# First quad's v brought to token order by four transfers from the scalar engine's queue instead of by TensorE, with all instructions in another order

## The chip, the cores and the metric

The kernel runs on one core of one Trainium2 chip. The metric is the device time of one execution in microseconds (us); less is better. The core has five instruction streams: TensorE (PE in the profile, its weight loads PEld), VectorE (DVE), ScalarE (ACT), GpSimd (POOL) and SyncE (SP). SP, ACT and POOL can each issue DMA transfers; the profile calls the DMA queue of SP q1, that of ACT q10 and that of POOL q0. Differences below about 0.3% (0.5 us) cannot be told from no change by a measurement of this kernel.

## The reference

```python
B, H, S, D = 4, 8, 768, 48
f = 1.0 / (1.0 + np.exp(-f_logit))
for t in range(S):
    state = f[:, :, t, :, None] * state + einsum('bhd,bhde', k[:, :, t], v[:, :, t])
    y[:, :, t] = einsum('bhd,bhde->bhe', q[:, :, t], state)
x = y.transpose(0, 2, 1, 3).reshape(3072, 384)
h = x @ w_in                       # 384 -> 2048
out = maximum(0.01 * h, h) @ w_out # 2048 -> 384
```

A gated linear attention over 768 tokens for four batches of eight heads is followed by a two-layer feed-forward block with a leaky ReLU.

## The kernel before

The sequence is cut into six chunks of 128 tokens. A chunk of one batch is a unit, numbered u = 4c + b, and the four units of a chunk are called a quad here. For each quad the kernel loads f, k, q and v, turns the gates into cumulated logarithms and from them into two factors, scales k and q by them, computes scores, masks them to the causal half, multiplies them with v ("mix"), adds the part that comes from the state, and updates the state. The result x of a unit feeds the feed-forward: `up` (x times w_in, L468, and L478 for later quads), the leaky ReLU on ScalarE (L473, L482), and `down` (times w_out, L486).

All instructions are written out by hand in one list of calls, in an order that holds for every engine: an engine runs its own instructions in the order of the list and waits on semaphores for what it needs. The DMA queue of an engine follows that engine's instructions. Tiles are fixed, with no allocator that could reorder anything.

The first quad is special. Its tokens are loaded interleaved: partition p holds batch p // 32 and four neighbouring tokens (32 times 4 = 128 tokens of a batch). Scaling and turning (`q_turn_pe`, `q_k_mul` and `q_q_mul`, L262 and L267) bring k and q into token order, and the scores come out in token order (`q_score_pe`, L281). The masks are made by VectorE (`q_mask`, L292), or by a ScalarE copy (`q_wf_act`, L285) and a GpSimd select (`q_mask_pool`, L288). v must be in token order too, 128 tokens of one batch on 128 partitions in tile `v_b`, before `q_mix_pe` (L307) and `state_pe` (L444) can use it. In the kernel before, two casts (`q_v_cast`) make v bf16, TensorE multiplies it for each batch with four 0/1 matrices `pick` (`q_pick`, L252: four matmuls for each batch, sixteen in all), and four copies (`q_v_out`) bring the result out of PSUM. Later quads use `cast_v` into the tile `vQ` and `v_dma`, one SBUF-to-SBUF transfer for each batch, from SP's queue (L391).

Calls to `idle_pe` put matmuls on zeros (L140) into PE's order where it has nothing to do; they are not part of the computation. `load_w_in` and `load_w_out` (L181, L186) load the feed-forward weights in four pieces each from POOL's queue, with a cast to bf16 on the way. `load_all` loads one chunk of an input, 768 KB, from SP's queue. `gate` is a one-element write that keeps a load from starting before its buffer is free.

Of the kernel before, what the change touches and what calls it, by code (L numbers as in the profile page):

```python
# [16 lines left out]
def kernel(  # L17
# [10 lines left out]
    nc = tc.nc  # L28
# [141 lines left out]
    def clear(eng, what):  # L170
        t = {"k": khQ[1][:, :, D:64], "q": qhQ[1][:, :, D:64], "v": vQ[:, :, :, D:64],
             "b": vbu[0][:, :, :, D:64]}[what]
        eng.memset(t, 0.0)
# [72 lines left out]

    def q_v_cast(eng, hh):
        move(eng, vqb[:, 4 * hh:4 * hh + 4], vq[:, 4 * hh:4 * hh + 4])

    def q_pick(b, bk):  # L250
        for i in range(4):
            nc.tensor.matmul(bank(bk)[:, 0:H * D].rearrange("p (h d) -> p h d", h=H),  # L252
                             pick[:, b, i].rearrange("p t j -> p (t j)"), vqb[:, :, i, :], start=(i == 0), stop=(i == 3))
# [132 lines left out]
    def cast_v(eng, c, hh):  # L386
        h = slice(4 * hh, 4 * hh + 4)
        move(eng, vQ[:, :, h, 0:D], v_raws[c % len(v_raws)][:, h].rearrange("p h j d -> p j h d"))

    def v_dma(c, b):  # L390
        nc.sync.dma_start(out=vbu[c % 2][:, b].rearrange("p h d -> p (h d)"),  # L391
                          in_=vQ[b::B].rearrange("p j h d -> p j (h d)"))
# [118 lines left out]
    clear(G, 'v')  # L511
    q_exp_act(0)
    q_exp_act(1)
# [3 lines left out]
    q_gate32(0, 0, 1, 2, 3)  # L517
    q_decay_b(0, emT, 1.0, 0, 0)
    idle_pe(2, 7)
    q_gate32(1, 0, 1, 2, 3)  # L520
    gate(G, fqs[0])
    gate(G, fqs[1])
    q_decay_b(1, emT, 1.0, 1, 0)
    q_k_cast(V, 0)
    load_all(fqs[1], f_logit, 1)
    q_decay_b(0, emT, 1.0, 0, 1)
    q_k_cast(V, 1)
    q_decay_b(1, emT, 1.0, 1, 1)
    idle_pe(4, 7)
    q_turn_pe(khq, 0, 4)  # L530
    load_all(fqs[0], f_logit, 2)
    q_decay_b(0, aT, -1.0, 0, 1)
    clear(V, 'b')
    q_decay_b(0, aT, -1.0, 0, 0)
    q_turn_pe(khq, 1, 5)
    q_k_mul(0, 1, 0, 4)
    q_decay_b(3, emT, 1.0, 3, None)
    q_k_mul(0, 0, 0, 4)
    q_decay_b(2, emT, 1.0, 2, None)
    q_k_mul(1, 0, 0, 5)  # L540
    q_q_cast(V, 1)
    q_q_cast(G, 0)
    q_decay_b(3, aT, -1.0, 3, None)
    q_k_mul(1, 0, 1, 5)
    q_decay_b(2, aT, -1.0, 2, None)
    idle_pe(11, 7)
    q_turn_pe(qhq, 1, 0)
    q_k_mul(0, 0, 1, 4)
    q_decay_b(1, aT, -1.0, 1, 0)
    touch('k')  # L550
    q_k_mul(1, 1, 1, 5)
    q_turn_pe(qhq, 0, 2)
    q_decay_b(1, aT, -1.0, 1, 1)
    q_k_mul(0, 1, 1, 4)
    q_q_mul(1, 1, 0, 0)
    q_back_pe(3, 4)
    q_q_mul(0, 1, 1, 2)
    q_back_pe(2, 1)
    q_v_cast(G, 0)
    q_v_cast(A, 1)  # L560
    q_q_mul(1, 0, 0, 0)
    q_q_mul(1, 1, 1, 0)
    q_q_mul(0, 0, 1, 2)
    q_q_mul(1, 0, 1, 0)
    load_w_in(1)
    idle_pe(8, 7)
    q_score_pe(0, 1, 3, 6)
    q_k_mul(1, 1, 0, 5)
    q_score_pe(1, 1, 0, 7)
    q_wf_act(0, 1, 1, 6)  # L570
    q_back_out(V, 3, 4)
    q_back_pe(1, 5)
    load_w_in(0)
    q_mask(0, 1, 0, 3)
    q_pick(1, 4)
    q_back_out(A, 2, 1)
    q_q_mul(0, 1, 0, 2)
    q_mask_pool(0, 1, 1)
    q_wf_act(1, 1, 1, 7)
    order_pe(3)  # L580
    q_q_mul(0, 0, 0, 2)
    q_pick(2, 1)
    q_mask(1, 1, 0, 0)
    load_w_in(2)
    q_v_out(A, 1, 4)
    g_exp(1, 0)
    q_score_pe(0, 0, 7, 2)
    q_v_out(V, 2, 1)
    q_score_pe(1, 0, 0, 4)
    q_mask_pool(1, 1, 1)  # L590
    q_pick(3, 6)
    order_out(3)
    q_wf_act(1, 0, 1, 4)
    load_w_in(3)
    clear(V, 'q')
    q_pick(0, 3)
    q_mask(0, 0, 0, 7)
    q_v_out(A, 3, 6)
    q_mask_pool(1, 0, 1)
    q_wf_act(0, 0, 1, 2)  # L600
    q_mix_pe(2, 4)
    gate(V, qqs[1])
    q_mask(1, 0, 0, 0)
    load_all(qqs[1], q, 1)
    q_mix_pe(3, 7)
    x_out(A, 2, 4)
    q_back_pe(0, 6)
    q_mask_pool(0, 0, 1)
    q_v_out(V, 0, 3)
    state_pe(3, 2)  # L610
    g_exp(2, 1)
    x_out(V, 3, 7)
    load_w_out(0)
    idle_pe(2, 1)
    q_mix_pe(1, 3)
    q_mix_pe(0, 4)
    g_exp(1, 1)
    q_back_out(V, 0, 6)
    up(1, 3, 7)
    x_out(V, 1, 3)  # L620
    g_ln(1, 0)
    x_out(V, 0, 4)
    up(1, 2, 6)
    q_back_out(V, 1, 5)
    g_exp(2, 0)
    up(0, 2, 4)
    q_state_dve(3)
    g_ln(2, 1)
    up(1, 0, 5)
    up(1, 1, 2)  # L630
    g_ln(1, 1)
    up(0, 3, 3)
    g_ln(2, 0)
    g_sum(V, 1, 1)
    up(0, 0, 0)
    up_act(1, 1, 2)
    g_sum(V, 1, 2)
    up(1, 5, 1)
    up_act(1, 3, 7)
    gate(V, kqs[1])  # L640
    g_sum(V, 1, 3)
    load_all(kqs[1], k, 1)
    up_act(1, 0, 5)
    up(0, 5, 2)
    g_sum(V, 2, 1)
    g_cast(G, 1)
    up_act(0, 3, 3)
    load_all(v_raws[0], v, 1)
    state_pe(1, 5)
    clear(V, 'k')  # L650
    up_act(0, 0, 0)
    g_pe(1, 7)
    g_sum(V, 2, 2)
    up(1, 4, 3)
    up_act(1, 5, 1)
    g_sum(V, 2, 3)
    up_act(0, 2, 4)
    state_pe(0, 0)
    up(0, 4, 1)
    up_act(1, 2, 6)  # L660
    g_add(1, 1, 7)
    g_cast(G, 2)
    up(0, 1, 4)
    up_act(0, 5, 2)
    load_w_out(1)
    q_state_dve(1)
    up_act(0, 4, 1)
    g_pe(2, 6)
    up(0, 6, 2)
    up_act(1, 4, 3)  # L670
    g_add(1, 0, 7)
    up_act(0, 1, 4)
    state_pe(2, 5)
    up(1, 6, 3)
    g_a(1, 1)
    q_state_dve(0)
    up(0, 7, 4)
    g_a(1, 0)
    q_state_dve(2)
    down(3, 0, 0)  # L680
    g_em(1, 0)
    g_q(V, 1, 0)
    q_state_pool(2)
    down(2, 0, 5)
    g_q(V, 1, 2)
    up_act(1, 6, 3)
    up(1, 7, 1)
    g_end(1, 7)
    q_state_pool(0)
    up_act(0, 6, 2)  # L690
    g_q(V, 1, 3)
    down(1, 0, 7)
    g_em(1, 1)
    g_q(V, 1, 1)
    t_pe(1, 1, 1, 2)
    q_state_pool(3)
    g_k(V, 1, 1)
    up_act(0, 7, 4)
    down(0, 0, 3)
    g_end(2, 6)  # L700
    g_k(V, 1, 0)
    up_act(1, 7, 1)
    t_pe(1, 1, 0, 4)
    load_w_out(2)
    t_out(A, 1, 1, 1, 2)
    g_k(V, 1, 3)
    t_pe(1, 0, 0, 1)
    load_w_out(3)
    g_add(2, 0, 6)
    down(2, 1, 5)  # L710
    t_out(A, 1, 0, 0, 1)
    down(3, 1, 0)
    g_k(V, 1, 2)
    t_out(V, 1, 1, 0, 4)
    kq_dma(1, 0, 3)
    t_pe(1, 0, 1, 2)
    cast_v(G, 1, 1)
    down(0, 1, 3)
    kq_dma(1, 0, 0)
# [641 lines left out]
```

## Time and profile before

| | |
|---|---|
| median of 3 runs | 175.36 us (175.34 to 175.89) |
| the profiled execution | 176.12 us, of which the span from the first to the last instruction is 174.4 us |
| PE busy | 168.3 us (96% of the span) |
| DVE busy | 109.2 us (63%) |
| ACT busy | 110.8 us (64%) |
| POOL busy | 49.9 us (29%) |
| moved by DMA | 37.53 MB, mean 215 GB/s |

The span is the profiled execution's time without what lies before its first and behind its last instruction, 1.7 us here. Busy matmuls on PE include those on zeros (10.3 us). In the timeline a row gives start, duration, engine, line, operation, output and input, the count, and in brackets the idle time just ahead of it with what ended it. In the DMA view a row gives a queue's packets, megabytes, and share of 16 engines' time in the stretch asked for.

### The profile page before, as it was taken

The page shows a single profiled execution, that of the slowest core. Times are in us where ns is not written, and L with a number is a line of the kernel's source. Part 1 is how long each engine was busy: PE and PEld are TensorE (multiplying, and loading weights), DVE is VectorE, ACT ScalarE, POOL GpSimd, SP SyncE. Part 2 cuts the span into 40 slices and gives each one's busy share as a digit, 9 for nine tenths or more (in the row PEclk, how much of TensorE's full clock was granted, in tenths as well). Part 3 has the DMA queues.
Part 4 walks back from the last instruction along what each step waited for, and adds up shares of the span by engine and source line. Part 5 has one row for each costly group of instructions (what it writes and reads, how often), then busy time and mean ns, then how long its engine had stood idle before and what let it go on. Part 6 is the DMA issues. An engine that isn't in the chain of part 4 may idle for free.

```text
span 174.4 us, 4660 instructions
## 1 busy us (share of the span) xinstructions
PE 168.3 (96%) x1896; PEld 108.4 (62%) x1896; DVE 109.2 (63%) x230; ACT 110.8 (64%) x201; POOL 49.9 (29%) x99
## 2 busy tenths in 40 slices
PE   7999999999999999999999999999999999999992
PEld 5776699866664566575555755555655566555572
DVE  7789959899766688966399768759470472020000
ACT  2786899994189997278982397790449703366531
POOL 7227803473003393000690002184038100000000
PEclk9999999999999999999999999999999999999999
DMA  5999999979499998999995999867699540007222
GB/s 152 302 327 319 198 208 296 317 126 233 126 344 331 333 235 164 346 260 355 212 237 146 341 240 300 238 165 242 165 282 195 157 167 4 0 0 272 89 92 93
DMA packets 52917, 37.53 MB, mean 215 GB/s; under 512 B 16416, under 2 KB 52384, under 8 KB 52896
## 3 DMA queue, kind: packets, MB, share of 16 engines
q1 hardware_dynamic: 50160, 33.69, 70.3%
q0 software_dynamic: 2176, 3.15, 10.6%
q10 hardware_dynamic: 560, 0.39, 0.8%
q8 instruction: 15, 0.25, 0.6%
q14 instruction: 6, 0.05, 0.1%
HBM read 25.17 MB, written 4.72 MB: 171 GB/s over the span
## 4 chain that ended last, share of the span: by engine, by line
PE 68%; ACT 9%; DMA 8%; DVE 7%; SPq 4%; issue 2%; POOL 0%; ACTq 0%; DVEq 0%
PE ps L486 29%; PE ps L478 24%; DMA qq<-in_q_dram 6%; ACT gT L473 3%; PE ps L420 3%; DMA fq<-in_f_logit_dram 2%; SPq L391 2%; PE ps L436 2%; PE ps L432 2%; PE ps L252 2%; PE ps L491 2%; DVE qhQ L377 1%; PE ps L444 1%; ACT fq L341 1%; ACT fq L337 1%
## 5 line engine op out<-in xcount | busy, mean ns | idle before, releaser
L486 PE MATMUL ps<-w_out_b,gT 128*128 128x384 bf16 x368 | 66.3, 326 | 0.0
L478 PE MATMUL ps<-xQ,w_in 128*128 128x512 bf16 x240 | 56.1, 379 | 0.4 <-ACT osb L146 0.4
L482 ACT ACTIVATE gT<-ps 128x512 bf16<-128x512 f32 x80 | 42.8, 611 | 17.2 <-PE ps L478 16.8
L486 PEld LDWEIGHTS <-gT 128*128 128x128 bf16 x368 | 34.4, 98 | 23.2
L478 PEld LDWEIGHTS <-w_in 128*128 128x128 bf16 x240 | 26.5, 113 | 21.8 <-issue 0.6
L424 DVE TENSOR_TENSOR wm<-ps,ut 128x512 bf16<-128x512 f32 x40 | 24.8, 682 | 12.0 <-ACT gT L482 6.8
L146 ACT CAST xQ<-ps 128x384 bf16<-128x384 f32 x14 | 6.1, 482 | 21.1 <-PE ps L436 21.0
L329 POOL CAST sb<-sf 64x192 bf16<-64x192 f32 x40 | 17.5, 436 | 4.9 <-DVE sf L323 2.5
L458 POOL TENSOR_TENSOR sf<-sf,a_end 128x192 f32<-128x192 f32 x16 | 9.3, 581 | 28.0 <-DVE sf L453 18.0
L146 ACT COPY osb<-ps 128x384 f32<-128x384 f32 (+1 forms) x15 | 6.8, 456 | 13.3 <-PE ps L486 8.6
L377 DVE TENSOR_TENSOR qhQ<-qq,a_t 128x384 bf16<-128x384 f32 x20 | 11.7, 617 | 2.0 <-DMA qq<-in_q_dram 1.6
L377 DVE TENSOR_TENSOR khQ<-kq,em_t 128x384 bf16<-128x384 f32 x20 | 11.8, 622 | 1.7 <-DMA kq<-in_k_dram 1.0
L361 DVE TENSOR_TENSOR fq<-fq,ps 128x768 f32<-128x768 f32 x10 | 9.4, 952 | 4.6 <-ACT gT L482 2.7
L468 PE MATMUL ps<-xQ,w_in 128*128 128x256 bf16 x96 | 11.5, 273 | 0.0
L140 PE MATMUL ps<-fill 128*128 128x256 bf16 x66 | 10.3, 318 | 1.1 <-DVE fill L97 1.1
L148 POOL CAST vQ<-v_raw 128x768 bf16<-128x768 f32 x8 | 6.9, 873 | 14.9 <-DMA v_raw<-in_v_dram 14.7
L148 DVE COPY osb<-ps 128x384 f32<-128x384 f32 x10 | 5.4, 554 | 9.0 <-PE ps L486 8.8
L345 DVE TENSOR_TENSOR fq<-fq 128x384 f32<-128x384 f32 x15 | 8.8, 592 | 2.7 <-issue 1.7
L148 POOL CAST lfq<-fq 128x384 bf16<-128x384 f32 x4 | 2.1, 529 | 29.1 <-ACT gT L482 16.6
L468 PEld LDWEIGHTS <-w_in 128*128 128x128 bf16 x96 | 10.1, 114 | 0.2
L452 DVE TENSOR_TENSOR sf<-sf,ps 64x192 f32<-64x192 f32 x16 | 5.5, 344 | 7.5 <-PE ps L444 7.2
L365 ACT ACTIVATE em_t<-fq 128x768 bf16<-128x768 f32 x10 | 8.7, 874 | 0.4 <-DVE fq L361 0.4
(100 smaller groups left out, 196.7 us busy)
## 6 DMA issues: line engine op xcount, KB each, us to landing
kq<-in_k_dram SPq DMA_DIRECT2D x6, 768.0 KB, 7.2
qq<-in_q_dram SPq DMA_DIRECT2D x6, 768.0 KB, 7.6
fq<-in_f_logit_dram SPq DMA_DIRECT2D x5, 768.0 KB, 7.3
v_raw<-in_v_dram SPq DMA_DIRECT2D x5, 768.0 KB, 6.3
out_dram<-osb SPq DMA_DIRECT2D x4, 768.0 KB, 4.0
kh<-khQ SPq DMA_DIRECT2D x20, 128.0 KB, 5.0
v_b<-vQ SPq DMA_DIRECT2D x20, 128.0 KB, 2.1
w_in<-in_moe_w_in_dram POOLq DMA_DIRECT2D x4, 384.0 KB, 7.6
```

The costliest lines, as they stand in the source:

```text
L140: nc.tensor.matmul(bank(bk)[:, 0:256], fill[:, 0:128], fill[:, 0:256], start=True, stop=True)
L146: eng.copy(out=out, in_=in_)
L148: eng.tensor_copy(out=out, in_=in_)
L329: nc.gpsimd.tensor_copy(out=state_b[b][r, :, e * D:(e + 1) * D], in_=state_f[b][r])
L361: nc.vector.tensor_add(t, t, x[:, :, None, :].to_broadcast([128, 4, 4, D]))
L377: eng.tensor_mul(out.rearrange("p (j g) d -> p j g d", j=4)[:, :, h, 0:D], raw[:, h].rearrange("p e j d -> p j e d"), by[:, h].rearrange(" ...
L424: nc.vector.tensor_mul(wms[e][u % R_WM], bank(bk).rearrange("p (i n) -> p i n", i=P2), ut[:, None, :].to_broadcast([128, P2, 128]))
L458: nc.gpsimd.tensor_mul(sf, sf, a_ends[c % 2][:, :, b:b + 1].to_broadcast([128, P2, D]))
L468: nc.tensor.matmul(bank(bk)[:, i * 256:(i + 1) * 256].rearrange("p (a n) -> p a n", a=2), w_in_p[ff // 4][:, kk, :, ff % 4], xQs[0][:, 2 * ...
L478: nc.tensor.matmul(bank(bk).rearrange("p (a n) -> p a n", a=B), w_in_p[ff // 4][:, kk, :, ff % 4], xQs[c % R_XT][:, :, kk, :], start=(kk = ...
L482: nc.scalar.activation(g_piece(c, ff), bank(bk), AF.Prelu, alpha=0.01)
L486: nc.tensor.matmul(bank(bk)[:, 0:KD], g_part(u, ff), w_out_b[:, ff, :], start=(ff == 0), stop=(ff == NF - 1))
```

## The change

The functions `q_v_cast`, `q_pick` and `q_v_out` go, and with them the tile `pick`, its building on GpSimd and VectorE, and the clearing of the padding of `v_b`. The first quad uses `cast_v` like the others, from the tile `vq`, and `v_dma` gets an argument for the issuing engine, which is ScalarE for the first quad. The list of calls is in another order throughout.

```diff
-    spare = gTs[GBUFS - 4].rearrange("p f a n -> p (f a n)")
-    vqb = spare[:, 2048:2048 + H * 4 * D].rearrange("p (h j d) -> p h j d", h=H, j=4)
-    pick = spare[:, 0:2048].rearrange("p (b i t j) -> p b i t j", b=B, i=4, j=4)
-    nc.gpsimd.memset(pick, 0.0)
-    for i in range(4):
-        nc.vector.tensor_copy(out=pick[:, :, i, :, i], in_=ident.rearrange("p (t b) -> p b t", b=B))
...
-    def q_v_cast(eng, hh):
-        move(eng, vqb[:, 4 * hh:4 * hh + 4], vq[:, 4 * hh:4 * hh + 4])
-
-    def q_pick(b, bk):
-        for i in range(4):
-            nc.tensor.matmul(bank(bk)[:, 0:H * D].rearrange("p (h d) -> p h d", h=H),
-                             pick[:, b, i].rearrange("p t j -> p (t j)"), vqb[:, :, i, :], start=(i == 0), stop=(i == 3))
-
-    def q_v_out(eng, b, bk):
-        move(eng, v_bs[b][:, :, 0:D], bank(bk)[:, 0:H * D].rearrange("p (h d) -> p h d", h=H))
...
     def cast_v(eng, c, hh):
         h = slice(4 * hh, 4 * hh + 4)
-        move(eng, vQ[:, :, h, 0:D], v_raws[c % len(v_raws)][:, h].rearrange("p h j d -> p j h d"))
-
-    def v_dma(c, b):
-        nc.sync.dma_start(out=vbu[c % 2][:, b].rearrange("p h d -> p (h d)"),
+        t = v_raws[c % len(v_raws)] if c else vq
+        move(eng, vQ[:, :, h, 0:D], t[:, h].rearrange("p h j d -> p j h d"))
+
+    def v_dma(c, b, eng=nc.sync):
+        eng.dma_start(out=vbu[c % 2][:, b].rearrange("p h d -> p (h d)"),
                           in_=vQ[b::B].rearrange("p j h d -> p j (h d)"))
...
+    load_w_out(0)
...
+    v_dma(0, 0, A)
+    q_q_mul(1, 1, 0, 1)
+    load_w_in(2)
```

ScalarE's instructions in the first quad, before, from its half of the cast of v on (`gT_173` and `gT_174` are the tiles lent to v, `wm` the masked scores, `v_b_160` v in token order for all four batches, `fq_72` the gates of the second chunk, `xQ_170` the x of the first quad):

```order
L146 CAST gT_173<-gT_174 128x768
L285 CAST wm_167<-ps_67 128x512
L146 COPY kh_154<-ps_62 128x512
L285 CAST wm_169<-ps_68 128x512
L146 CAST v_b_160<-ps_65 128x8x48
L337 ACTIVATE fq_72<-fq_72 128x768
L285 CAST wm_168<-ps_65 128x512
L146 CAST v_b_160<-ps_67 128x8x48
L285 CAST wm_166<-ps_63 128x512
L146 CAST xQ_170<-ps_65 128x384
```

The same stretch of ScalarE in the changed kernel:

```order
L146 CAST vQ<-gT_174 128x4x4x48
L267 CAST wm_167<-ps_63 128x512
L374 DMA v_b_160<-vQ 128x1x512 x2
L267 CAST wm_166<-ps_67 128x512
L374 DMA v_b_160<-vQ 128x1x512 x2
L267 CAST wm_168<-ps_67 128x512
L267 CAST wm_169<-ps_63 128x512
L319 ACTIVATE fq_72<-fq_72 128x768
L323 ACTIVATE fq_72<-fq_72 128x768
L146 CAST xQ_170<-ps_65 128x384
```

The four transfers stand between the copies of the scores, the first two behind the first copy; both gate activations of the second chunk now stand ahead of the copy of x.

GpSimd's instructions before, from the building of the constants on (`four` is a small constant, `gT_173` in its second appearance the target of the cast of v, `w_in_100` to `w_in_102` pieces of the first weights):

```order
L209 COPY four<-ident 4x128
L213 MEMSET gT_173 128x2048
L173 MEMSET vQ 128x32x16
L166 CAST fq_71<-ident 128x1
L166 CAST fq_72<-ident 128x1
L148 CAST qhQ_111<-qq_75 128x16x48
L177 COPY seen<-kq_73 128x1
L148 CAST gT_173<-gT_174 128x768
L181 DMA w_in_101<-in_moe_w_in_dram 128x3x512
L181 DMA w_in_100<-in_moe_w_in_dram 128x3x512
```

The same stretch of GpSimd in the changed kernel:

```order
L208 COPY four<-ident 4x128
L185 DMA w_out_b<-in_moe_w_out_dram 128x1536
L148 CAST khQ_109<-kq_73 128x16x48
L166 CAST fq_72<-ident 128x1
L176 COPY seen<-kq_73 128x1
L148 CAST qhQ_111<-qq_75 128x16x48
L180 DMA w_in_101<-in_moe_w_in_dram 128x3x512
L148 CAST vQ<-gT_174 128x4x4x48
L180 DMA w_in_100<-in_moe_w_in_dram 128x3x512
L180 DMA w_in_102<-in_moe_w_in_dram 128x3x512
```

The first piece of w_out stood behind the masks of the first quad, as the fifth weight load; it is now the first transfer of POOL's queue, right behind the constants. GpSimd also takes over half of the cast of k.

On TensorE the calls between the gate matmuls and the first `up` hold, before, four score steps, four turns, four `q_back_pe`, sixteen pick matmuls, four mixes, one state step and 27 matmuls on zeros; in the changed kernel the picks are gone, all four state steps stand there, and 37 matmuls on zeros. The calls of PE behind the first `up` are the same in kind and number in both, but for the three state steps.

More of the change, by code (lines that the diff above doesn't have):

```diff
@@ L517 @@
     q_gate32(0, 0, 1, 2, 3)
+    order_pe(4)
     q_decay_b(0, emT, 1.0, 0, 0)
[L519 to L534 removed]
@@ new lines @@
+    g_a(4, 1)
+    mask(12, 1, 4)
+    down(10, 0, 2)
+    g_exp(5, 1)
+    mask(12, 0, 6)
+    down(8, 3, 0)
+    mask(13, 1, 5)
+    g_ln(5, 1)
+    state_pe(14, 6)
+    mix_pe(12, 4)
+    state_dve(14)
+    put(A, 8, 0)
+    mix_pe(13, 5)
+    g_em(4, 1)
+    mix_pe(15, 7)
+    g_sum(V, 5, 1)
+    mix_pe(14, 6)
+    x_out(A, 12, 4)
+    x_out(V, 15, 7)
+    down(10, 1, 2)
+    cast_v(G, 4, 1)
+    g_end(4, 3)
+    x_out(A, 13, 5)
+    g_sum(V, 5, 2)
+    x_out(A, 14, 6)
+    down(11, 3, 1)
+    g_sum(V, 5, 3)
```

1461 lines of the change are left out of this document (721 added, 740 removed).

## Prediction

> **What bounds the kernel now.** I read the page first, then TensorE's waits, then the timelines of the first 24 us, engine by engine, then the DMA view in short stretches. The page, and TensorE's waits from 22 us to the end (us in total, times, longest):
>
> ```profile
> PE 168.3 (96%) x1896; PEld 108.4 (62%) x1896; DVE 109.2 (63%) x230; ACT 110.8 (64%) x201; POOL 49.9 (29%) x99
> PE ps L408 <- DVE khQ L377: 0.5, 1, 0.5
> PE ps L478 <- ACT osb L146: 0.4, 1, 0.4
> ```
>
> TensorE is busy 96% of the span, and from the first `up` on it waits 0.9 us in all. So the end is the start of the first `up` plus a fixed amount of matmuls. That start is set by the first quad, of which TensorE's timeline shows these rows:
>
> ```profile
> 8.90 0.63 PE L233 MATMUL ps<-steps,lfq 32*128 32x128 bf16 x32
> 16.48 0.81 PE L252 MATMUL ps<-gT 128*128 128x384 bf16 x4
> 17.38 0.82 PE L252 MATMUL ps<-gT 128*128 128x384 bf16 x4
> 18.69 1.47 PE L252 MATMUL ps<-gT 128*128 128x384 bf16 x8
> 21.37 0.63 PE L307 MATMUL ps<-wm,v_b 128*32 128x128 bf16 x32
> 21.94 6.08 PE L468 MATMUL ps<-xQ,w_in 128*128 128x256 bf16 x54
> ```
>
> The first `up` starts at 21.94. The three pick rows are 3.1 us of TensorE's time ahead of it (0.81 + 0.82 + 1.47). What feeds the first quad are loads; these rows of VectorE, GpSimd and ScalarE show when they arrive:
>
> ```profile
> 8.61 1.03 DVE L148 CAST khQ<-kq 128x768 bf16<-128x768 f32 x2 [1.10 <-DMA kq<-in_k_dram]
> 11.03 0.83 POOL L148 CAST qhQ<-qq 128x768 bf16<-128x768 f32 x1 [2.90 <-DMA qq<-in_q_dram]
> 13.44 0.83 POOL L148 CAST gT<-gT 128x768 bf16<-128x768 f32 x1 [1.12 <-DMA gT<-in_v_dram]
> 13.40 0.86 ACT L146 CAST gT<-gT 128x768 bf16<-128x768 f32 x1
> 9.55 4.00 ACT L238 ACTIVATE gT<-ps 128x256 f32<-128x256 f32 x11 [0.71 <-PE ps L233]
> ```
>
> k, q and v arrive at 8.6, 11.0 and 13.4, 2.4 us apart, and each cast waits for its load. DMA is the scarce thing here. Its share of 16 engines' time is the next to last number of these rows (us, and busy us with counts of PE, PEld, DVE, ACT and POOL ahead of it):
>
> ```profile
> 10.90:13.40 2.50, 2.23 (x28) 1.73 (x25) 2.50 (x8) 2.50 (x7) 1.28 (x2) 1.00 1.12 331
> 16.00:20.00 4.00, 3.97 (x42) 2.10 (x37) 3.88 (x13) 3.58 (x8) 3.25 (x5) 1.00 1.21 239
> ```
>
> It is 1.12 and 1.21, so it is full: every byte that is put ahead makes another later.
>
> **The change: TensorE.** The picks go, 3.1 us of TensorE's work. It is no gain by itself, since TensorE waits for other things in its place, and 37 matmuls on zeros stand there now instead of 27. So I sum by the start of the first `up`. Of the state steps, three more now lie ahead of it; each is four matmuls, by this row of the chain
>
> ```profile
> 77.13 0.17 PE ps L444 x4
> ```
>
> 0.17 us, so what follows the first `up` is 0.5 us shorter. For what else is reordered behind it I take nothing: TensorE's calls there are the same, and the other engines hide behind it as they do now. If that cover fails, or gets better, it is of the size of the 0.9 us above, either way.
>
> **The change: the load of w_out.** It was issued at 21.17, and now follows the constant `four` on GpSimd, which ends at 2.9:
>
> ```profile
> 2.65 0.28 POOL L209 COPY four<-ident 4x128 bf16<-4x128 bf16 x1
> 21.17 0.58 POOL L186 DMA_DIRECT2D w_out_b<-in_moe_w_out_dram  x1
> 2.99 0.66 SPq L73 DMA_DIRECT2D qq<-in_q_dram  x1
> 4.52 1.73 SPq L73 DMA_DIRECT2D gT<-in_v_dram  x1
> q0 software_dynamic: 1127, 1.11, 118.1%
> q1 hardware_dynamic: 1733, 1.31, 109.6%
> ```
>
> The next two rows are SP's issues of q and v, behind that of k. The last two rows are POOL's queue from 18 to 24 us, nearly alone, and SP's queue from 9 to 13 us, alone (packets, MB, share). POOL's moves 0.185 MB per us, so 384 KB take 2.1 us of all engines. k was handed to its queue before 2.99, q at 2.99, about when GpSimd gets there, and v at 4.52. I take k as it is, and q and v 2.1 us later: 13.1 and 15.5. The bounds are nothing (it fits in where the engines are not full) and 2.1 us for k as well.
>
> **The change: VectorE's list.** Its rows, and what TensorE and ScalarE take for scores, x and a pair of gate activations:
>
> ```profile
> 11.63 0.64 DVE L148 CAST qhQ<-qq 128x768 bf16<-128x768 f32 x1
> 13.59 2.08 DVE L267 TENSOR_TENSOR qTs<-ps,gT 128x256 bf16<-128x256 bf16 x6
> 15.92 0.42 DVE L148 COPY kh<-ps 128x512 bf16<-128x512 bf16 x1
> 16.25 0.68 DVE L292 TENSOR_TENSOR wm<-ps,ut 128x512 bf16<-128x512 f32 x1
> 18.20 0.55 PE ps L281 x16
> 15.84 0.59 ACT L285 CAST wm<-ps 128x512 bf16<-128x512 f32 x1 [1.58 <-PE ps L281]
> 20.56 0.48 ACT L146 CAST xQ<-ps 128x384 bf16<-128x384 f32 x1
> 20.93 1.58 ACT L337 ACTIVATE fq<-fq 128x768 f32<-128x768 f32 x2
> ```
>
> A multiply is 2.08 / 6 = 0.35. q's cast ends at 13.1 + 0.64 = 13.75; thirteen multiplies stand behind it. The seventh, at 16.2, releases the first score step (0.55, to 16.75) and its copy on ScalarE (0.59, to 17.35). Behind the twelfth (17.95) come a mask (0.68), a copy (0.42) and the thirteenth multiply: 19.4. The last score step ends at 19.95, and a mask, a copy and two masks end at 19.95 + 3 × 0.68 + 0.42 = 22.4. Then TensorE runs two mixes (0.57, from the row at 21.37 to the next), two matmuls on zeros (0.2) and two state steps (0.34): the first `up` at 23.5 if v and x are there by then.
>
> **The change: the four transfers.** v arrives at 15.5, and its casts (0.86) end at 16.35. ScalarE's list has the first copy of scores ahead, so the first transfer is issued at 17.35. Queued behind it on ScalarE are the other three copies of scores, for which GpSimd's masks wait, two gate activations, and the copy of the first x, for which `up` waits. With 0.6 an issue (the row below) that is 17.35 + 4 × 0.6 + 3 × 0.59 + 1.58 + 0.48 = 23.6, 0.1 behind VectorE's list. So even with v there at once the first `up` would be at 23.6, 1.7 later than now, 1.2 with the 0.5 taken off. The trace has such transfers on SP's queue only (durations of the issue, then issue to landing, both min, median, max), and these rows show two queues at once, from 25 to 28 us, and the first w_in, issued at 14.20, in the stretch from 14 to 17:
>
> ```profile
> L391 SPq DMA_DIRECT2D v_b<-vQ x20: 524/603/1727, 41.5 to 137.5; - x20
> DMA to landing us min/median/max: 2.0/2.1/5.6
> q0 software_dynamic: 250, 0.46, 81.5%
> q1 hardware_dynamic: 316, 0.24, 29.9%
> 14.20 1.73 POOL L181 DMA_DIRECT2D w_in<-in_moe_w_in_dram  x2
> q1 hardware_dynamic: 1261, 0.95, 105.5%
> q0 software_dynamic: 20, 0.02, 4.0%
> ```
>
> From 25 to 28 the packets are 250 to 316: two busy queues take turns, about packet by packet. One transfer of v is 128 packets of 1 KB, 8 on each of 16 engines. An engine's packet costs 16 × 6 / 1127 = 0.085 us on POOL's queue and 16 × 4 / 1733 = 0.037 on SP's. For one of ours, SBUF to SBUF, I take 0.05, between the two. While w_in (POOL) and the gates of chunks 2 and 3 (SP) are moving, a turn is 0.17 us. The three w_in pieces (2.1 each) and two gate loads (2.4 each) are 11 us of DMA behind v at 15.5, so both stay busy to the end of it. The four transfers are 32 turns: 5.4 us. The fixed part is 2.1 less 8 × 0.05, 1.7 us. So the last v lands at 17.35 + 1.7 + 5.4 = 24.45, against 22.7 at which its mix is due. The last mix, zeros and states are 0.82, and the first `up` starts at 25.27. **The sum:** 25.27 − 21.94 = 3.3, less 0.5: 2.8 us slower. The profiled execution of 176.12 us (its span of 174.4 and 1.7 around it) would become 178.9; the median of the runs shown, 175.36, is 0.76 lower, and so 178.2.
>
> Its bounds: with q and v not delayed, everything starts 2.0 earlier (the exponentials of the row at 9.55 hold VectorE there until about 11.7, against 13.75), which gives 23.27 and +0.8, 176.2. Above, the w_in row gives 1.2: issued at 14.20, with a fixed part of 1.7 it would start at 15.9, but only 20 of its packets went by 17, while SP's queue had 1261. With that and 0.9 for the rest, 180.3.
>
> **The rivals.** *The transfers are hidden:* they land 2.1 after issue, as the median of 20 has it, the last at about 21.9, ahead of its mix. Then ScalarE's list decides, and the time is 175.36 + 1.2 = 176.6. For it: small packets in a queue of their own. Against: the DMA share of 1.21. *Faster:* the same, and w_out costs q and v nothing. Both lists then end 2.0 earlier, the first `up` comes at 21.6 and 0.5 falls away: −0.8, 174.6. It decides if the last v lands before 20.8, that is if a transfer takes about 3 us or less although three queues are moving. For it speaks that DMA is empty before 2 us, and that w_out's place might be filled with other waiting; against it the casts, each of which waits for its load now. *A new queue waits for what older ones have already been given:* then the transfers begin 1.2 later, as that w_in did; the first `up` comes at 26.5, +4.0, 179.4.
>
> On this last one there is a rule: the Trainium skill, page "DMA: Bandwidth & Descriptors", section "Queues, rings and completion order", says that each DMA engine goes round-robin between the queues that have work, a packet at a time. By that rule the late start would not be, and the sum would be the 178.2. The packets from 25 to 28 us agree with it, the 20 against 1261 from 14 to 17 us do not.
>
> **How the numbers follow.** Chances: the forecast 0.45, late start 0.17, transfers hidden 0.15, faster 0.23. The first alone spans 176.2 to 180.3. For 8 in 10 the range must reach over the hidden transfers and most of the faster case, to 174.3 with a part of the 0.9 for the rest, and it leaves out the upper part of the late start: 174.3 to 180.3. About 0.3%, 0.5 us, is what a measurement can tell from no change. Of the faster case a small part, and of the hidden transfers another, falls within it: faster 0.21, same 0.05, slower 0.74.
>
> **What would show it.** Right: in the changed kernel's TensorE timeline the state and mix rows ahead of the first `up` carry waits for DMA into `v_b`, the transfers take 3 to 7 us to landing, q's and v's casts start near 13 and 15.5, and the first `up` starts near 25. Wrong: q's cast at 11, transfers of 2 us, and a first `up` before 22; or new waits of TensorE behind it that exceed 0.9 us, for which I have no term.

## The result and the profile after

The changed kernel takes 183.07 us (median of 6 runs, 182.63 to 184.92) against 175.45 us for the kernel before on the same chip (174.78 to 176.31, 6 runs): ratio 1.0456, 95% interval 1.0396 to 1.0516. It is slower, as forecast, but by 7.6 us and not by 2.8, and above the range. (Ratios, here and below, leave disturbed executions out, medians do not.) The profiled execution took 182.8 us with a span of 180.8 us; before it was 176.12 and 174.4. So the spans differ by 6.4 us, and this is what the rows below have to account for.

TensorE on the page, and three of its waits over the whole span (us in total, times, longest):

```profile
PE 169.0 (93%) x1890; PEld 109.3 (60%) x1890; DVE 107.4 (59%) x227; ACT 110.7 (61%) x197; POOL 46.7 (26%) x96
PE ps L427 <- DMA v_b<-vQ: 3.5, 2, 2.9
PE ps L461 <- ACT gT L465: 1.6, 1, 1.6
PE ps L427 <- DVE sf L436: 0.7, 1, 0.7
```

TensorE's busy time is the same to 0.7 us; it waits. The first row of waits lies ahead of the first `up`, the other two at 87.1 and 66.4 us. Behind the first `up` TensorE now waits 2.3 us where it waited 0.9. Its timeline around the first `up`:

```profile
19.33 0.83 PE L140 MATMUL ps<-fill 128*128 128x256 bf16 x6
23.06 0.34 PE L427 MATMUL ps<-v_b,kh 128*128 128x96 bf16 x4 [2.90 <-DMA v_b<-vQ]
24.18 0.48 PE L427 MATMUL ps<-v_b,kh 128*128 128x96 bf16 x4 [0.56 <-DMA v_b<-vQ]
25.01 1.99 PE L289 MATMUL ps<-wm,v_b 128*32 128x128 bf16 x64
27.67 6.71 PE L451 MATMUL ps<-xQ,w_in 128*128 128x256 bf16 x60
```

The first `up` starts at 27.67, against 21.94 before and 25.27 forecast. At 20.2 TensorE comes to the first state step in its list, and is held there until v's first transfer has landed. The arrival of k, q and v, and the transfers (durations of the issue and its times; issue to landing, min, median, max):

```profile
10.65 0.56 DVE L148 CAST khQ<-kq 128x768 bf16<-128x768 f32 x1 [5.35 <-DMA kq<-in_k_dram]
13.09 1.21 POOL L148 CAST qhQ<-qq 128x768 bf16<-128x768 f32 x1 [0.95 <-DMA qq<-in_q_dram]
15.93 0.83 POOL L148 CAST vQ<-gT 128x768 bf16<-128x768 f32 x1 [0.91 <-DMA gT<-in_v_dram]
L374 ACTq DMA_DIRECT2D v_b<-vQ x4: 595/608/618, 16.8 to 18.8; - x4
DMA to landing us min/median/max: 6.2/6.7/7.6
```

The first transfer is issued at 16.81 and each takes 6.2 to 7.6 us to land. What the queues moved in the meantime (packets, MB, share of 16 engines), from 17 to 20 us, from 20 to 21, and then from 21 to 23:

```profile
q1 hardware_dynamic: 834, 0.63, 69.9%
q0 software_dynamic: 224, 0.23, 45.6%
...
q0 software_dynamic: 198, 0.19, 118.2%
q10 hardware_dynamic: 8, 0.01, 3.0%
q1 hardware_dynamic: 8, 0.01, 2.5%
...
q0 software_dynamic: 251, 0.25, 74.0%
q10 hardware_dynamic: 239, 0.23, 41.6%
```

This is the core of the case. From 17 to 20 us the transfers' queue q10 has no row at all: SP's q1, with the gates, gets 834 packets and POOL's q0, with w_in, 224. At 20 to 21, over three microseconds after the first transfer was issued, q10 gets 8 packets through while q0 gets 198. From 21 on the two take turns, 239 to 251. The transfers did not share the engines from the start; here they began about when the one w_in piece that had been handed over ahead of them, 400 packets, was through.

### The profile page after: what moved, and what is told of

Same layout as the page of the kernel before. It is cut to its first block, busy times and chain, and to the rows that moved or that the text cites. A ratio compares the mean times of both kernels' runs of the same rounds, so it can differ in the third digit from the quotient of the medians.

```text
span 180.8 us, 4649 instructions
## 1 busy us (share of the span) xinstructions
PE 169.0 (93%) x1890; PEld 109.3 (60%) x1890; DVE 107.4 (59%) x227; ACT 110.7 (61%) x197; POOL 46.7 (26%) x96
## 3 DMA queue, kind: packets, MB, share of 16 engines
q0 software_dynamic: 2176, 3.15, 10.0%
## 4 chain that ended last, share of the span: by engine, by line
PE 65%; DMA 20%; issue 6%; DVE 3%; SPq 2%; ACT 2%; POOL 0%; ACTq 0%; POOLq 0%
PE ps L469 29%; PE ps L461 21%; DMA gT<-in_v_dram 6%; DMA qq<-in_q_dram 6%; DMA v_b<-vQ 4%; PE ps L451 3%; DMA v_raw<-in_v_dram 3%; PE ps L403 3%; DMA fq<-in_f_logit_dram 2%; PE ps L427 2%; PE ps L391 2%; PE ps L419 1%; PE ps L474 1%; SPq L379 1%; PE ps L415 1%
## 5 line engine op out<-in xcount | busy, mean ns | idle before, releaser
L148 DVE COPY osb<-ps 128x384 f32<-128x384 f32 (+1 forms) x14 | 7.5, 540 | 25.3 <-PE ps L469 24.5
L311 POOL CAST sb<-sf 64x192 bf16<-64x192 f32 x40 | 16.6, 415 | 18.5 <-PE ps L415 8.7
L146 ACT COPY osb<-ps 128x384 f32<-128x384 f32 (+1 forms) x11 | 5.1, 471 | 19.8 <-PE ps L469 17.0
L146 ACT CAST xQ<-ps 128x384 bf16<-128x384 f32 x15 | 6.6, 482 | 12.8 <-PE ps L419 8.8
L140 PE MATMUL ps<-fill 128*128 128x256 bf16 x76 | 12.9, 327 | 1.1 <-DVE fill L97 1.1
L359 DVE TENSOR_TENSOR khQ<-kq,em_t 128x384 bf16<-128x384 f32 x20 | 11.4, 602 | 4.3 <-ACT em_t L347 2.3
L359 DVE TENSOR_TENSOR qhQ<-qq,a_t 128x384 bf16<-128x384 f32 x20 | 12.0, 650 | 2.4 <-DMA qq<-in_q_dram 2.4
L427 PE MATMUL ps<-v_b,kh 128*128 128x96 bf16 x80 | 6.7, 209 | 4.2 <-DMA v_b<-vQ 3.5
L140 PEld LDWEIGHTS <-fill 128*128 128x128 bf16 x76 | 8.3, 116 | 3.7 <-DVE fill L97 1.1
L148 POOL CAST vQ<-v_raw 128x768 bf16<-128x768 f32 x6 | 5.3, 877 | 20.3 <-DMA v_raw<-in_v_dram 12.9
L427 PEld LDWEIGHTS <-kh 128*128 128x128 bf16 x80 | 5.4, 100 | 7.6 <-DMA v_b<-vQ 3.2
```

The costliest lines, as they stand in the source:

```text
L140: nc.tensor.matmul(bank(bk)[:, 0:256], fill[:, 0:128], fill[:, 0:256], start=True, stop=True)
L146: eng.copy(out=out, in_=in_)
L148: eng.tensor_copy(out=out, in_=in_)
L311: nc.gpsimd.tensor_copy(out=state_b[b][r, :, e * D:(e + 1) * D], in_=state_f[b][r])
L359: eng.tensor_mul(out.rearrange("p (j g) d -> p j g d", j=4)[:, :, h, 0:D], raw[:, h].rearrange("p e j d -> p j e d"), by[:, h].rearrange(" ...
L427: nc.tensor.matmul(pt[:, p, :], kh[:, 2 * p:2 * p + 2, :], v_b[:, 2 * p:2 * p + 2, 0:D], start=True, stop=True)
```

## The experiments

Every kernel ran beside the kernel before, and its ratio is to that kernel's runs on the same chip (medians 175.7 to 176.0).

**Only the transfers, in before's order** (`b_vdma`). Four transfers on ScalarE's queue, two behind each of the first two copies of scores, replace the four picks and their copies; the loads and the rest of the list stay.

```diff
     q_wf_act(0, 1, 1, 6)
+    v_dma(0, 2, A)
+    v_dma(0, 3, A)
...
-    q_pick(1, 4)
...
     q_wf_act(1, 1, 1, 7)
+    v_dma(0, 1, A)
+    v_dma(0, 0, A)
...
-    q_pick(2, 1)
...
-    q_pick(3, 6)
...
-    q_pick(0, 3)
```

> The kernel before, in its own order, with the first quad's v brought over by four transfers from ScalarE's queue; the picks and their copies are left out, the rest stands as it was. Theory A (the transfers wait for earlier loads and take turns with w_in): issued near 16.4, they land 4 to 7 us after issue, TensorE waits for v_b 2 to 4 us, its clock falls to 0.50 for a stretch, the first up starts at 25 to 27 instead of 21.94, and the time is 179 to 182 us. Rival B (it is the other order of the instructions that costs): the time is within 1 us of before, 174.5 to 176.5.

180.89 us, ratio 1.0309 (1.0253 to 1.0365). Queues from 17 to 20 us, and TensorE's first `up`:

```profile
q0 software_dynamic: 525, 0.52, 114.9%
q10 hardware_dynamic: 1, 0.00, 0.1%
...
26.96 7.39 PE L469 MATMUL ps<-xQ,w_in 128*128 128x256 bf16 x54
```

The transfers are issued from 15.9 to 17.8, and one of their packets passes before 20. The same late start, with nothing else of the change: the transfers alone cost 5.2 us here. Not all of it need be the late start, since the 54 matmuls of `up` take 7.39 us where they took 6.08: the mean granted clock of this execution is 0.971, and it is 0.50 from 20 to 28 us.

**Only the early load of w_out, in before's order** (`b_wout`).

```diff
+    load_w_out(0)
     nc.gpsimd.memset(pick, 0.0)
...
-    load_w_out(0)
```

> The kernel before with one edit: the first piece of w_out is issued right behind the constants, at 2.9 instead of 21.2. Theory A holds the load to cost a part: k, q and v arrive about 2 us later, the first up starts 1.0 to 1.8 later, and the time is 176.3 to 177.3 us. Rival C (the early load is the main cost): 4 us or more, 179.5 and above. If it costs nothing: 175.4.

177.13 us, ratio 1.0103 (1.0048 to 1.0158). VectorE's cast of k, and the first `up`:

```profile
10.32 1.03 DVE L148 CAST khQ<-kq 128x768 bf16<-128x768 f32 x2 [2.09 <-DMA kq<-in_k_dram]
23.66 6.33 PE L469 MATMUL ps<-xQ,w_in 128*128 128x256 bf16 x54
```

k comes 1.7 us later than in the kernel before, and so does the first `up`.

**The changed kernel with picks in place of the transfers** (`a_pick`). The picks and their copies stand behind the last score step.

```diff
-    v_dma(0, 0, A)
...
-    v_dma(0, 3, A)
...
     q_score_pe(1, 0, 1, 6)
+    q_pick(0, 7)
+    q_pick(1, 3)
...
+    q_pick(2, 0)
...
+    q_pick(3, 2)
```

> The changed kernel with the picks in place of the four transfers: v goes through TensorE as before, the load of w_out stays early and the order stays but for the picks, which take the place of eight matmuls on zeros. Theory A: no wait of TensorE for DMA ahead of the first up, clock 1.00 throughout, first up at 23.5 to 25, time 177.5 to 179.5 us. Rival B: what is lost is lost in the order, and the time stays within 1.5 us of the change, 181.5 and above.

179.51 us, ratio 1.025 (1.0172 to 1.0329): of the 7.6 us, 3.6 go with the transfers. TensorE's picks, its first `up`, and its waits far behind it:

```profile
18.84 2.77 PE L248 MATMUL ps<-gT 128*128 128x384 bf16 x16
24.09 6.87 PE L465 MATMUL ps<-xQ,w_in 128*128 128x256 bf16 x60
PE ps L475 <- ACT gT L479: 1.7, 1, 1.7
PE ps L441 <- DVE sf L450: 0.7, 1, 0.7
```

The two later waits are there without the transfers: they come with the new lists.

**The changed kernel with TensorE kept busy in its wait** (`a_warm`).

```diff
-    idle_pe(6, 7)
+    idle_pe(33, 7)
     state_pe(0, 3)
...
-    idle_pe(2, 7)
+    idle_pe(7, 7)
     state_pe(1, 0)
```

> The changed kernel with 32 more matmuls on zeros in TensorE's waits for the first two transfers (27 more ahead of the first state step, 5 more ahead of the second), about 3.4 us of them, so that TensorE is busy while it waits. Theory A, with the fallen clock as a part of its own: the clock stays at 1.00, the mixes take 1.2 instead of 1.9, and the time is 1.0 to 1.6 us under the change, 181.5 to 182. If the clock's fall costs nothing: 183, or more if the matmuls on zeros outlast the wait.

182.84 us, ratio 1.0429 (1.0366 to 1.0491), not to be told from the changed kernel. In the changed kernel the windows from 22 to 28 us show the granted clock (third number from the end), which falls after the wait of 2.9 us:

```profile
22.00:24.00 2.00, 0.56 (x6) 0.38 (x7) 0.00 (x0) 0.15 (x1) 0.07 (x1) 0.97 1.19 245
24.00:26.00 2.00, 1.82 (x48) 1.62 (x51) 0.25 (x1) 0.00 (x0) 0.00 (x0) 0.50 1.20 234
26.00:28.00 2.00, 2.00 (x50) 1.51 (x39) 1.99 (x6) 1.86 (x3) 0.00 (x0) 0.67 1.22 204
```

With the zeros the mean clock of the whole span is 0.999 and the mixes run at full speed, but they meet v instead:

```profile
24.89 0.33 PE L427 MATMUL ps<-v_b,kh 128*128 128x96 bf16 x4 [0.81 <-DMA v_b<-vQ]
26.82 0.41 PE L289 MATMUL ps<-wm,v_b 128*32 128x128 bf16 x16 [0.60 <-DMA v_b<-vQ]
27.73 6.71 PE L451 MATMUL ps<-xQ,w_in 128*128 128x256 bf16 x60
```

The slow clock cost nothing in the profiled execution; the landing of the last v sets the first `up`. Three of the six executions of the changed kernel have a mean clock of 0.980 or 0.981 and take 183.14 to 184.92 us, the other three 0.991 and 182.63 to 183.0; whether the half clock reached into `up` in the former, no trace shows.

**What do the transfers wait for?** Three kernels start from before's order with the transfers, and each alters one thing. The first takes three w_in loads from their places and hands them over behind the transfers and two of GpSimd's masks (`b_vdma_win`):

```diff
-    load_w_in(1)
...
-    load_w_in(0)
...
-    load_w_in(2)
...
     q_mask_pool(1, 1, 1)
+    load_w_in(1)
+    load_w_in(0)
+    load_w_in(2)
```

> Before's order with the four transfers in place of the picks, and the three w_in loads that GpSimd issues ahead of the first masks moved behind those masks, so that they are handed over after the transfers (issued about 15.9 to 17.8) and not before. Theory (a transfer that is handed over later doesn't start until what was handed over before it has moved): the transfers now stand only behind the second gate load, whose packets end near 17.5; issue to landing about 2 to 4 us instead of 6.7 to 8.6, the last v near 20 to 21, the first up no longer set by v but by w_in or the lists, 22 to 24.5, time 175.5 to 178. Rival (the lateness is the transfers' own: a fixed time and ScalarE's queue): landing stays at 6 to 8 us, the first up stays near 27, time near 181.

The second hands the second gate load, on SP's queue, over behind them (`b_vdma_f2`):

```diff
-    gate(G, fqs[0])
-    load_all(fqs[0], f_logit, 2)
...
     load_w_in(2)
+    gate(G, fqs[0])
+    load_all(fqs[0], f_logit, 2)
```

> Before's order with the four transfers in place of the picks, and the second gate load (1.5 MB less the first chunks, on SP's queue) handed over behind them and not before; w_in stays where it was. Theory (backlog of work handed over before): about 2.4 us less stands ahead, so the transfers land 4 to 6 us after issue instead of 6.7 to 8.6, and the first up comes at 24 to 25. Rival (own fixed time): landing as in the kernel without this move, 6.7 to 8.6. The gate activations behind the load may be late, so the time says little.

The third issues the transfers on SP's queue (`b_vdma_sp`):

```diff
-    v_dma(0, 2, A)
-    v_dma(0, 3, A)
+    v_dma(0, 2)
+    v_dma(0, 3)
...
-    v_dma(0, 1, A)
-    v_dma(0, 0, A)
+    v_dma(0, 1)
+    v_dma(0, 0)
```

> Before's order with the four transfers in place of the picks, issued on SP's queue and not on ScalarE's. Theory (the lateness is work handed over before, on whatever queue): the transfers still wait for the second gate load and w_in, TensorE still waits for v about 3.5 to 4.5 us, the first up between 26 and 27.7, time 180 to 182. Rival (a queue of its own, new to this stage, is what is late): on SP's queue, which is moving already, they land within 3 to 5 us, the first up is 23 to 24.5, time 177 to 178.5.

The times are 180.49 us (ratio 1.0294, 1.0233 to 1.0354), 190.26 us (one run) and 180.79 us (1.0279, 1.0216 to 1.0342). The transfers in the DMA view (KB each, median us from issue to landing), one row from each kernel in the same order, then the queues of the second kernel from 17 to 20 us, those of the third from 18 to 19, and the third's first `up`:

```profile
v_b<-vQ ACTq DMA_DIRECT2D x4, 128.0 KB, 2.6
...
v_b<-vQ ACTq DMA_DIRECT2D x4, 128.0 KB, 8.4
...
v_b<-vQ SPq DMA_DIRECT2D x4, 128.0 KB, 6.4
...
q0 software_dynamic: 405, 0.40, 105.9%
...
q0 software_dynamic: 148, 0.15, 115.9%
q1 hardware_dynamic: 19, 0.02, 4.5%
...
24.93 8.55 PE L469 MATMUL ps<-xQ,w_in 128*128 128x256 bf16 x54
```

With w_in behind them the transfers land in 2.6 us. With SP's load out of the way they still take 8.4: SP's queue is empty there, q0 runs alone, and q10 has no row at all, though the transfers are issued from 16.1 on. So it is w_in, on POOL's queue, that they wait for; my expectation of 4 to 6 us for that kernel was wrong. On SP's queue the transfers were issued 1.4 us earlier, from 14.5, at about the time of the first w_in. One of them, 144 packets, has passed by 19 us; the others are held back here too, 19 packets to 148 from 18 to 19, and take turns from 19 on, 109 to 104 up to 20. The first `up` came at 24.93, between what theory and rival expected and 2.0 us earlier than in `b_vdma`, yet the time is the same: its 54 matmuls take 8.55 us against 7.39 there, 1.2 of the 2.0.

The time of the first of the three does not fall with the landing. TensorE's first `up` there, GpSimd's w_in, and two windows (granted clock, DMA share and GB/s at the end):

```profile
24.69 4.03 PE L469 MATMUL ps<-xQ,w_in 128*128 128x256 bf16 x18
19.15 3.27 POOL L181 DMA_DIRECT2D w_in<-in_moe_w_in_dram  x4
16.00:18.00 2.00, 0.89 (x14) 0.58 (x13) 2.00 (x6) 1.16 (x3) 0.64 (x1) 1.00 0.76 236
20.00:22.00 2.00, 1.73 (x41) 1.53 (x41) 1.22 (x3) 1.76 (x4) 2.00 (x4) 0.50 0.42 47
```

The clock is at 0.50, and issuing w_in, from 19.15 to 22.42, holds GpSimd's other masks back. A fourth kernel, `b_vdma_win_warm`, puts seven matmuls on zeros at each place where a pick was:

```diff
+    idle_pe(7, 4)
...
+    idle_pe(7, 1)
...
+    idle_pe(7, 6)
...
+    idle_pe(7, 3)
```

> The kernel with before's order, the transfers, and w_in behind them, with seven matmuls on zeros standing at each of the four places where a pick stood (28 in all, some 3.0 us at the full clock). Theory: without the picks TensorE waits ahead of the first up, its granted clock falls to 0.50 from about 19 to 29 us, and this costs 2.1 us in the first 54 up matmuls (8.4 us against 6.1) and a part of the 2.75 us by which their start is late; with the zeros the clock stays at 1.00, the 54 take 6.1 to 6.4 us, and the time is 177 to 178.5. Rival (the late start of w_in and the masks behind it cost the time, the clock follows): the clock stays, and the time stays at 180 to 180.8.

181.69 us, ratio 1.0355 (1.0292 to 1.0419). The rival's time, and a little more. The clock is 1.00, and the matmuls of `up` wait 1.6 us for w_in instead, most of it here:

```profile
27.71 2.81 PE L469 MATMUL ps<-xQ,w_in 128*128 128x256 bf16 x24 [1.09 <-DMA w_in<-in_moe_w_in_dram]
```

So with w_in put last TensorE waits for w_in, and with the clock at full the time is no less. The engines were not full throughout, though: their share is 0.42 from 20 to 22 us in the row above, with w_in handed over from 19.15 on. A kernel that hands it over right behind the last transfer, issued at 18.1, was not run.

**The parts of the change in its own order.** First the picks again, and w_out's load at its old place (`a_order`), then the transfers with w_out's load at its old place (`a_wout_late`):

```diff
-    load_w_out(0)
...
     load_w_in(3)
+    load_w_out(0)
```

> The changed kernel with the picks instead of the transfers and with w_out's load at its old place: only the other order of the instructions is left of the change. Theory (the parts add up: transfers 3.6, w_out 1.4 to 1.7, order what remains): k at 8.6, the first up at 22.1 to 22.6, the two waits of 1.6 and 0.7 us on gT and sf behind it stay; 177.0 to 177.8. Rival 1 (those waits come of the early w_out): they go, 175.2 to 175.8. Rival 2 (the order is better and the early load hid it): under 175.

> The changed kernel with w_out's load back behind the fourth w_in, as before the change. Theory (transfers start only when w_in that was handed over before is done, and they alone set the first up): k, q, v at 8.6, 11, 13.5, w_in and the transfers are issued 2 us earlier, all loads ahead of them are 2.1 us of DMA less, so the last v lands 1.5 to 2.2 us earlier, the first up at 25.5 to 26.2; 181 to 181.7. Rival (the half clock appears with a longer wait, as in before's order with the transfers): 182 to 183.

179.82 us (ratio 1.0217, 1.0176 to 1.0259) and 182.49 us (1.0355, 1.0297 to 1.0412). With picks the place of w_out's load makes no difference that can be told (1.0217 against 1.025). With transfers the late load is 0.6 us better by the medians and 1.0% by the ratios, and less than was expected. In the first of the two kernels VectorE reaches its half of q late, at 12.56, and the picks stand in a row as in the kernel with the early load, so that the first `up` comes at 24.31; the last row is the first `up` of the second kernel:

```profile
19.06 2.77 PE L248 MATMUL ps<-gT 128*128 128x384 bf16 x16
...
26.33 6.71 PE L451 MATMUL ps<-xQ,w_in 128*128 128x256 bf16 x60
```

I had expected the parts to add up. With the picks in a row behind the last score step, these two kernels do not show what the order alone costs. Next, w_out late and w_in behind the transfers (`a_win`):

```diff
-    load_w_in(1)
...
-    load_w_in(0)
...
-    load_w_in(2)
...
     q_mask_pool(0, 0, 1)
+    load_w_in(1)
+    load_w_in(0)
+    load_w_in(2)
```

> The changed kernel with w_out's load at its old place and with the w_in loads of 1, 0 and 2 moved behind the first mask on GpSimd, so that they are handed over behind the transfers. Theory: the transfers land in 2 to 3 us and no longer set the first up; the lists do, at 22 to 23.5, or w_in; with the waits of 1.6 and 0.7 behind it, 177 to 178.5, 4.5 to 6 us better than the changed kernel. Rival (w_in now comes late, or the clock halves for 10 us): 179.5 to 181.5.

185.59 us, ratio 1.0536 (1.0459 to 1.0613), above what theory and rival expected. No wait for v is left, and the first `up` comes at 23.70, but issuing w_in holds the masks back again, and late loads cost more behind:

```profile
PE ps L334 <- POOL lfq L148: 2.8, 1, 2.8
PE ps L289 <- POOL wm L270: 1.5, 1, 1.5
```

To take w_in out of the transfers' way without touching any list, the next kernel leaves three of its four loads out (`a_nowin`), and another has w_out's load late besides (`a_wl_nowin`):

```diff
+    for g in (1, 0, 2):
+        nc.gpsimd.memset(w_in_b[g], 0.0)
...
-    load_w_in(1)
...
-    load_w_in(0)
...
-    load_w_in(2)
```

> The changed kernel without three of the four w_in loads (numbers 1, 0 and 2; GpSimd writes zeros into their tiles before 10 us instead, so up multiplies by zeros there): nothing that GpSimd hands over stands ahead of the transfers, and no engine's list is altered otherwise. Theory (the wait of 3.5 us for v and the late first up at 27.7 are those loads, handed over before the transfers): each transfer lands 2 to 3 us after its issue, the waits for v fall under 0.5 us, and the first up comes when the lists let it, 23.3 to 24.5; time 179 to 180. Rival (transfers from SBUF to SBUF on ScalarE's queue are slow by themselves, or wait for the gate loads): the first up stays past 26.

> As the kernel without the three w_in loads, and w_out's load is back at its old place behind the fourth w_in. It shows what the early w_out costs once the transfers hide nothing. The prediction's list has q 2.1 us earlier and so the first up 2.0 earlier: 21.4 to 22.4, time 177 to 178. Rival (VectorE reaches q's cast at about 12 anyway, as in the kernel with picks, where the load's place made no difference): the first up within 0.8 of the kernel with the early load, and the times within 0.8.

180.42 us (ratio 1.0223, 1.0144 to 1.0302) and 178.81 us (1.016, 1.0113 to 1.0208). The wait for v and the first `up` of the first, then the first `up` of the second, which has no such wait:

```profile
21.42 0.34 PE L427 MATMUL ps<-v_b,kh 128*128 128x96 bf16 x4 [1.09 <-DMA v_b<-vQ]
24.13 6.88 PE L451 MATMUL ps<-xQ,w_in 128*128 128x256 bf16 x60
...
21.95 6.87 PE L451 MATMUL ps<-xQ,w_in 128*128 128x256 bf16 x60
```

This divides up the first stage. Without the three w_in loads and without the early w_out, the changed lists reach the first `up` at 21.95, as the kernel before did at 21.94. The early w_out adds 2.2 us (24.13), and the three w_in loads 3.5 more (27.67). These 3.5 are all that the loads cost there, the transfers' late start, their turns with w_in and GpSimd's time to issue it; these runs do not separate them. With w_in loaded, w_out's place moves the first `up` by 1.3 only (26.33). The wait of 1.09 that is left, where I expected under 0.5, is beside the gate loads on SP's queue; the transfers land 4.1 us after issue there. In the second kernel they are issued from 15.46 on; the queues there from 16.8 to 17.0:

```profile
q10 hardware_dynamic: 38, 0.04, 59.8%
q1 hardware_dynamic: 46, 0.03, 50.6%
```

So beside SP's queue at work the transfers begin 1.3 us after their issue and take turns at once. SP's queue does not hold them back; w_in on POOL's does. The second kernel's 178.81 with an unmoved first `up` leaves 2.8 us to what lies behind.

**The two waits behind the first `up`.** ScalarE's cast of the fourth quad's v waits for its load until 85.7 us, and the gT that TensorE needs stand behind it; VectorE's first scaling of the third quad's q (a multiply, L359) does the same to the sums `sf`. `a_tail` moves both back:

```diff
-    g_q(V, 2, 3)
...
+    g_q(V, 2, 3)
     g_q(V, 2, 1)
...
-    cast_v(A, 3, 0)
     up4(2, 6, 1)
     up4_act(2, 0, 0)
     v_dma(3, 3)
...
     up4_act(2, 6, 1)
+    cast_v(A, 3, 0)
```

> The changed kernel with two casts moved back in the lists, behind the first up: ScalarE's cast of the fourth quad's v behind two gT (it waits for its load until 85.7, and TensorE waits 1.6 us for the gT behind it), and VectorE's first cast of the third quad's q behind the sums for the state (it waits for its load 2.4 us, and TensorE waits 0.7 for sf). Theory (the order of the new list, not the transfers, makes these two waits): both go, nothing replaces them, 2.3 us less than the changed kernel: 180.3 to 181.3. Rival (the loads themselves are late and TensorE meets the next wait on them): a gain under 0.8, 182.3 to 183.

187.76 us, ratio 1.0676 (1.0627 to 1.0726). This was my mistake: in the list the cast now stands behind the transfers that read its tile, so they move the old values, the cast has to wait for them, and the run says nothing on the question. `a_tail2` moves the two transfers along:

```diff
     up4_act(2, 6, 1)
+    cast_v(A, 3, 0)
+    v_dma(3, 3)
+    v_dma(3, 2)
```

> The changed kernel with two casts moved back behind the first up, and nothing else on any engine: ScalarE's cast of the fourth quad's v behind two gT, ahead of the transfers that read it, and VectorE's first cast of the third quad's q behind the sums for the state. Theory (the place of the two casts makes the two later waits): the waits of 1.6 us on gT and 0.7 on sf go and nothing replaces them, 2.3 us less than the changed kernel: 180.3 to 181.3. Rival (the loads that the casts wait for are late, and TensorE meets the next wait on them): a gain under 0.8 us, 182.3 to 183.

183.80 us, ratio 1.0378 (1.0313 to 1.0442); by the ratios 0.8% or 1.4 us less than the changed kernel, with intervals that overlap. Its waits behind the first `up`:

```profile
PE ps L403 <- DMA qTs<-qh: 0.9, 1, 0.9
PE ps L469 <- DVE sf L436: 0.3, 1, 0.3
PE ps L391 <- DVE sf L436: 0.2, 1, 0.2
```

The wait of 1.6 for gT is gone and that for `sf` smaller, but 1.4 us of others are there: 0.9 us less than 2.3. Its profiled execution, 184.94 us, was one of its longer ones, with the first `up` at 28.28, so its waits tell more than its span. The answer lies between theory and rival. The place of the cast makes the larger of those waits and that of the scaling at least a part of the smaller, and more than half comes back, 0.9 us of it as a wait for the next late transfer.

**A better version of the kernel before?** The prediction found TensorE waiting for other things. `b_pick2` uses that wait for two of the four picks:

```diff
-    idle_pe(8, 7)
+    q_pick(1, 7)
+    q_pick(2, 6)
```

> The kernel before with its picks by TensorE; two of the four (b=1 and b=2) are moved into TensorE's wait for VectorE at 14.1 to 15.4, in place of 8 matmuls on zeros. If that wait is free, 1.6 us of picks leave the stretch ahead of the first up, which then is set by the scores and comes 0.7 to 1.6 earlier: 173.9 to 174.8. If the masks and scores already set it (the picks fill waits): 175.0 to 175.8, no change. If the picks' copies on ScalarE push the first wm back: up to 0.6 slower.

176.19 us, ratio 1.0031 (1.0001 to 1.0061): no gain. The first `up` comes at 21.82, since the scores then wait 0.8 us for ScalarE's copy. No kernel here beats the one before.

## Why the prediction was wrong

**The direction and the bound held.** The end is the first `up` plus a fixed amount of work. The first `up` moved by 5.7 us; three state steps moved ahead of it, 0.5; the waits behind it grew by 1.4: 6.6, against 6.4 measured between the spans.

**The step that failed first is the start of the transfers**, "The fixed part is 2.1 less 8 × 0.05, 1.7 us". It takes the landing of a transfer on a nearly idle queue and adds turns with the other queues from then on. The issue was forecast well (17.35, measured 16.81). The turns came out near, 5.4 us against some 5, nearly all of the packets passing from 21 to 26, but in part by luck: the sum has 32 turns of 0.17 us with SP's gate loads in each, and there were 36 (the four are 576 packets, and not 512) of 0.13, with 13 packets of SP's from 21 to 23. But from issue to the turns it took 4.2 us and not 1.7. The 1.7 is not too small where w_in is missing: beside SP's queue alone the first packets pass after 1.3. The prediction had the evidence of more: the first w_in, 20 packets against 1261, which it priced at 1.2 us as a rival with a chance of 0.17. That rival was the mechanism, and 1.2 was too small: from the one case of w_in it took the size for the transfers, where it is 4.2 less 1.7, 2.5. The kernel that puts w_in behind the transfers (2.6 us to landing) and those without it show that w_in is the cause. The last v lands at about 26.8, where the kernel with zeros ends its wait, against 24.45 forecast; that is the 2.4 by which the first `up` is later than 25.27. The turn-taking rule of the Trainium skill, page "DMA: Bandwidth & Descriptors", section "Queues, rings and completion order", agrees with the rows from 21 us on and not with those before, in which q10, with transfers issued over three microseconds earlier, gets 8 packets to 198; the measurement decides.

**Then the slow clock came on top, and cost nothing in the profiled execution.** It has no term in the prediction, and the kernel with zeros shows that none was missing there. In before's order with the transfers it reaches into `up` (7.39 and 8.55 us against 6.08). The windows give its length: (0.03 + 0.50 + 0.33) × 2 / 0.5 = 3.4 us. In the kernel that puts w_in behind the transfers, with 0.61 from 18 to 20 us, 0.50 to 28 and 0.83 to 30, it is 10.2, three times as long. The Trainium skill, page "TensorE: Matmul & The Clock Gate", section on the HAM clock gate, has the clock set by free-running windows of about 3.4 us, back to full only after a busy one; both lengths agree.

**The early w_out** delayed q as forecast (13.1; measured 13.09), v a little more (15.9 for 15.5), and k by 2.0 us where the forecast left it alone: its bound, "2.1 us for k as well", was the truth. The lists' 23.6 without a wait for v stands well beside the measured 24.13, of which some is a wait for v.

**The rest behind the first `up`**, "I take nothing" (±0.9), is the second failed step: 1.4 us of new waits. The larger, on gT, is there in every profiled kernel with the new lists that leaves that cast in its place, from 1.1 to 1.8 us, with transfers and with picks. They come of a cast and a scaling that wait for a load with work behind them that TensorE needs. The prediction compared TensorE's calls only; it did not look at what stands behind a waiting cast on ScalarE and VectorE. That the place makes them was shown for the larger one, and how much of the time they are worth was not settled, as their removal brought other waits.

**The rest of the miss** is which execution was profiled: that of before lay 0.76 us above the median that the forecast used, that of after 0.27 below its own, 1.0 us together. The 4.9 us are 2.4 in the first `up`, 1.4 behind it, and this 1.0.

The other rivals fell: no transfer was hidden, though in the kernel without w_in and with the late w_out they are, and even there it is 178.8 us, because of what lies behind.

## What to carry over

Before moving work from an engine to a transfer, look at what has been handed to the DMA engines ahead of it, on every queue, and not at the landing time of such a transfer at rest: here 2.1 us became 6.7. Where the DMA share is full, putting one load behind another moves the wait to that load, and handing it over late leaves the engines partly idle first (0.42 here). Matmuls that filled a wait of TensorE were not a cost to be saved. With an order written by hand, ask of every instruction that waits for a load what stands behind it on its engine.

## What the runs showed of the hardware

A queue with nothing in it got almost nothing through while GpSimd's queue worked off w_in that had been issued before: 1 packet to 525 in 3 us (transfers on ScalarE's queue), and turns of 1 to 1 from then on. It did not depend on SP's queue being busy, and SP's queue alone did not do it: 38 packets to 46 in the kernel without three w_in loads and with the late w_out, about 1.5 us after the issue.

What ends the hold stays open. A w_in piece is 400 packets (q0 moves 2176 in all, and 976 without three pieces). When the turns begin, q0 has moved 422 in the changed kernel, by 21 us, with one piece handed over ahead of the transfers; 554 in `b_vdma`, by 20, with two ahead, 800; and 238 by 19 where the transfers are on SP's queue. That the work handed over earlier must be done first fits the first of these and not the others. The w_in pieces handed over beside the transfers and behind them, from 16.70 on in the changed kernel, take turns with them.

Half clock needs no long wait. In the changed kernel it follows one of 2.9 us; in the kernel with w_in behind the transfers no wait of TensorE is over 1.1 us, but it is busy only 0.89 of 2 us from 16 to 18, and the clock then stays at half for 10.2 us although TensorE is busy 1.73 of 2 us from 20 to 22.
